# Batch 0 of an attention kernel: side blocks in pairs, one panel per output, the z and v of batch 1 fetched later, weights fetched in runs

## The chip, the core and the metric

The kernel runs on one core of a Trainium2 chip. The metric is the device time of one execution in microseconds (us). Before the change it was 1002.39 us, the median of three runs (1002.05 to 1003.09).

## The reference, cut to what matters

There are 8 batches of 3136 rows. The attention stage, which the change touches, is:

```python
scores = scale * np.matmul(z, z.transpose(0, 2, 1))   # z: 8 x 3136 x 64, scale = 1/3136
attn = np.maximum(scores, 0.0) ** 2
x = u * np.matmul(attn, v)                            # u, v: 8 x 3136 x 256
# after it, per batch: a rank-32 mixing over the rows, then relu(x @ w1) @ w2 over the channels
```

## The kernel before

The 3136 rows are 24 blocks of 128 and a tail of 64: 25 "outputs", made in the order 12 to 24, then 0 to 11. The matrix of squared scores is symmetric, so that only half of each row of blocks is computed (a "panel", thirteen blocks wide). The other half comes from panels of earlier outputs, transposed by the DMA engines into a "strip". All strips go through one queue (the sync queue), and so does the transposed copy of z for the next batch. In the trace it issues them one after another (a strip from 36.25 to 38.47 us, the two parts of z from 38.59 to 41.92, the next strip at 42.02): this is what "in-order queue" means in the prediction.

A panel part is scored on TensorE in PSUM (the memory of its results), taken out ("evicted") with a relu by ScalarE and squared by VectorE:

```python
def score(b, parts):
    ps = pair_psum()
    for k, (j, c, n, _) in enumerate(parts):
        mm(out=ps[:, k, :n], lhsT=zT[halves[k], j, :], rhs=zT_flat[halves[k], c : c + n], ...)
    # ... one or two evictions ...
    for dst, src in todo:
        nc.scalar.activation(out=dst, in_=src, func=AF.Relu, scale=sc)
    for dst, _ in todo:
        nc.vector.tensor_tensor(out=dst, in0=dst, in1=dst, op=ALU.mult)

def turn(b, o):                         # the strip of output o; five buffers
    strip = strip_pool.tile([P, HALF, P], BF16, name="strip")
    transpose(out=strip, in_=A[o][:, P:])
    strips[b, o] = strip
```

There is one array A of panels for all batches. A score of batch 1 therefore overwrites a panel of batch 0, and may do so only when everything that reads the old panel has read it, the DMA transposes among them.

Batch 0 has a start of its own, in which outputs 12 to 19 are begun before all of z is there. Its last part looks like this; the two calls in the middle are z of batch 1:

```python
rest = []
for j in reversed(range(FIRST - NG, LEAD)):                 # FIRST = 12, LEAD = 16, NG = 4
    rest += score_steps(0, j, LEAD + NG - j, NB)            # the side blocks, panel by panel
for i, pair in enumerate(pairs):
    # ...
    use_stored(pair, outs)
    if B > 1 and i in (1, 2):
        part = ((0, FIRST), (FIRST, NF))[i - 1]
        double_z(1, (part,))                                # copies on VectorE
        turn_z(1, (part,))                                  # DMA transpose on the sync queue
```

After it, tables say which panel is scored beside which output (index i is output (12 + i) mod 25, `next_at` is for the batch after), and where the loads of v of the next batch go:

```python
first_at = {8: [(NT - 2, 0, NB), (0, 0, NB)], 9: [(NT - 1, 0, NB)], 10: [(1, 0, NB)]}
first_at.update({11: [(2, 0, NB)], 12: []})
for j, i in zip(range(3, FIRST), (10, 11, 11, 12, 12, 12, 12, 12, 12)):
    first_at[i].append((j, 0, FIRST - j))
# ...
v_at = dict(zip((9, 11, 13, 15, 18, 21), V_PARTS[3:]))
```

## Time and profile before

| | before |
|---|---|
| time, median of 3 runs | 1002.39 us |
| the profiled run | 1000.08 us, span 998.3 us |
| granted TensorE clock | 1.00 |
| TensorE busy | 983.4 us, 99 % |
| idle time of TensorE | 14.9 us |

The columns are: the stretch, its length, then busy time with count of PE (TensorE), PEld (its weight loads), DVE (VectorE), ACT (ScalarE) and POOL (GpSimd), the granted TensorE clock as a share of full speed, the share of the DMA engines (the time of all packets over that of 16 engines; packets overlap, so that it can pass 1), and GB/s.

### The profile page before, as it was taken

The page shows a single profiled execution, that of the slowest core. Times are in us where ns is not written, and L with a number is a line of the kernel's source. Part 1 is how long each engine was busy: PE and PEld are TensorE (multiplying, and loading weights), DVE is VectorE, ACT ScalarE, POOL GpSimd, SP SyncE. Part 2 cuts the span into 40 slices and gives each one's busy share as a digit, 9 for nine tenths or more (in the row PEclk, how much of TensorE's full clock was granted, in tenths as well). Part 3 has the DMA queues.
Part 4 walks back from the last instruction along what each step waited for, and adds up shares of the span by engine and source line. Part 5 has one row for each costly group of instructions (what it writes and reads, how often), then busy time and mean ns, then how long its engine had stood idle before and what let it go on. Part 6 is the DMA issues. An engine that isn't in the chain of part 4 may idle for free.

```text
span 998.3 us, 31020 instructions
## 1 busy us (share of the span) xinstructions
PE 983.4 (99%) x13688; PEld 776.5 (78%) x13688; DVE 551.1 (55%) x1003; ACT 612.2 (61%) x835; POOL 171.7 (17%) x317
## 2 busy tenths in 40 slices
PE   8899999999999999999999999999999999999998
PEld 6678777787778877788787887878877788787866
DVE  6878754467444665456644566445664457542352
ACT  8877764667645776466754667556674666643154
POOL 5111112111121211221112211112111120011000
PEclk9999999999999999999999999999999999999999
DMA  9999989899798999999999997989979998678533
GB/s 195 185 195 204 174 156 186 185 176 173 153 198 171 169 157 186 179 178 169 160 180 176 181 168 149 188 174 177 175 151 194 166 188 159 120 150 161 129 95 101
DMA packets 414790, 167.94 MB, mean 168 GB/s; under 512 B 389488, under 2 KB 399408, under 8 KB 414656
## 3 DMA queue, kind: packets, MB, share of 16 engines
q1 hardware_dynamic: 385424, 99.68, 62.3%
q0 software_dynamic: 29232, 66.28, 28.3%
q8 instruction: 107, 1.75, 0.7%
q14 instruction: 27, 0.22, 0.1%
HBM read 61.88 MB, written 25.69 MB: 88 GB/s over the span
## 4 chain that ended last, share of the span: by engine, by line
PE 91%; DVE 4%; ACT 3%; DMA 1%; issue 1%; POOL 0%; DVEq 0%; POOLq 0%
PE ps L371 47%; PE ps L563 17%; PE ps L610 17%; PE ps L298 6%; ACT A L311 2%; DVE A L313 2%; PE ps L405 1%; PE ps L531 1%; DVE x_bf L545 1%; DMA out_dram<-o_sb 1%; DMA strip<-A 1%; DVE both L386 1%; PE ps L479 1%; DVE x_bf L395 1%; PE ps L207 0%
## 5 line engine op out<-in xcount | busy, mean ns | idle before, releaser
L311 ACT ACTIVATE A<-ps 128x832 bf16<-128x832 f32 (+9 forms) x477 | 358.9, 769 | 155.4 <-PE ps L298 148.1
L371 PE MATMUL ps<-v,A 64*128 64x256 bf16 x4988 | 341.6, 269 | 1.8 <-DVE A L313 1.1
L313 DVE TENSOR_TENSOR A<-A 128x832 bf16<-128x832 bf16 (+9 forms) x477 | 244.7, 527 | 133.1 <-ACT A L311 130.0
L371 PE MATMUL ps<-v,strip 64*128 64x256 bf16 x4420 | 307.3, 269 | 3.4 <-DMA strip<-A 2.5
L371 PEld LDWEIGHTS <-A 64*128 64x128 bf16 x4988 | 246.3, 94 | 45.4 <-issue 10.0
L581 ACT ACTIVATE relu_bf<-ps 128x1024 bf16<-128x1024 f32 (+2 forms) x206 | 186.2, 911 | 140.0 <-PE ps L563 139.8
L371 PEld LDWEIGHTS <-strip 64*128 64x128 bf16 x4420 | 222.6, 94 | 37.2 <-DMA strip<-A 3.9
L624 DVE TENSOR_TENSOR o_sb<-ps,x_bf 128x512 f32<-128x512 f32 (+2 forms) x105 | 69.9, 665 | 243.7 <-PE ps L610 221.7
L610 PE MATMUL ps<-w_bf,relu_bf 128*128 128x256 bf16 (+1 forms) x1600 | 201.2, 273 | 0.0
L563 PE MATMUL ps<-ut,w_bf 128*128 128x512 bf16 (+2 forms) x896 | 198.6, 353 | 0.0
L610 PEld LDWEIGHTS <-relu_bf 128*128 128x128 bf16 (+1 forms) x1600 | 153.0, 98 | 45.6 <-issue 3.6
L563 PEld LDWEIGHTS <-w_bf 128*128 128x128 bf16 x896 | 84.9, 98 | 62.0 <-issue 6.9
L355 POOL DMA_DIRECT2D u_sb<-in_u_dram x96 | 53.7, 559 | 456.1 <-DVE x_bf L395 441.9
L298 PE MATMUL ps<-zT 64*128 64x416 bf16 (+8 forms) x812 | 131.6, 312 | 0.0
L385 ACT COPY both<-ps 128x512 f32<-128x512 f32 (+1 forms) x104 | 58.9, 566 | 72.9 <-PE ps L371 66.6
L637 POOL DMA_DIRECT2D out_dram<-o_sb x84 | 46.0, 548 | 276.2 <-DVE o_sb L624 272.9
L386 DVE TENSOR_TENSOR both<-ps,both 128x512 f32<-128x512 f32 (+1 forms) x104 | 69.3, 667 | 28.2 <-ACT both L385 27.5
L395 DVE TENSOR_TENSOR x_bf<-both,u_sb 128x512 bf16<-128x512 f32 (+1 forms) x104 | 69.8, 672 | 3.7
L545 DVE TENSOR_TENSOR x_bf<-ps,x_bf 128x512 bf16<-128x512 f32 (+1 forms) x112 | 65.5, 626 | 7.2 <-PE ps L531 7.1
L298 PEld LDWEIGHTS <-zT 64*128 64x128 bf16 x812 | 43.1, 94 | 4.0
L244 POOL DMA_DIRECT2D v<-in_v_dram x61 | 34.1, 561 | 0.8 <-DMA w_bf<-in_moe_w_ch_dram 0.7
L298 PE MATMUL ps<-relu_bf 64*128 64x416 bf16 (+9 forms) x121 | 22.2, 333 | 3.9 <-ACT A L311 3.3
(54 smaller groups left out, 208.0 us busy)
## 6 DMA issues: line engine op xcount, KB each, us to landing
u_sb<-in_u_dram POOLq DMA_DIRECT2D x96, 256.0 KB, 4.1
out_dram<-o_sb POOLq DMA_DIRECT2D x84, 256.0 KB, 3.3
v<-in_v_dram POOLq DMA_DIRECT2D x57, 192.0 KB, 4.8
strip<-A SPq DMA_TRANSPOSE x196, 5.5
out_dram<-o_sb SPq DMA_DIRECT2D x11, 256.0 KB, 2.0
z_c<-in_z_dram POOLq DMA_DIRECT2D x7, 384.0 KB, 5.9
u_sb<-in_u_dram POOLq DMA_DIRECT2D x16, 64.0 KB, 2.5
ut<-x_bf SPq DMA_TRANSPOSE x56, 3.7
```

Of the source, the lines that this page charges most:

```text
L298: mm(out=ps[:, k, :n], lhsT=zT[halves[k], j, :], rhs=zT_flat[halves[k], c : c + n], start=True, stop=True,)
L311: nc.scalar.activation(out=dst, in_=src, func=AF.Relu, scale=sc)
L313: nc.vector.tensor_tensor(out=dst, in0=dst, in1=dst, op=ALU.mult)
L371: mm(out=acc[t0][h][:, (o - t0) * D : (o - t0 + 1) * D], lhsT=w[halves[h]], rhs=v_both[b % 2][halves[h], j, :], start=start, stop=stop, **kw,)
L385: nc.scalar.copy(out=both[:, :w], in_=banks[1][:, :w])
L386: nc.vector.tensor_tensor(out=both[:, :w], in0=banks[0][:, :w], in1=both[:, :w], op=ALU.add)
L395: nc.vector.tensor_tensor(out=x_at(b, t0, n), in0=split(both[:, :w]), in1=u_sb[:, :n, :].rearrange("p t (a c) -> p t a c", c=P), op=ALU.mult,)
L545: nc.vector.tensor_tensor(out=q, in0=split(ps[h][:, : len(ks) * D]), in1=q, op=ALU.add)
L563: mm(out=ps[i][:, :w] if apart else ps[:, i, :w], lhsT=w1_bf[:, db, (hp + i) * P : (hp + i + 1) * P], rhs=uT[c][:, db, len(chunks[c]) * P ...
L581: nc.scalar.activation(out=relus[c][:, hp : hp + 2, :w], in_=ps[:, :, :w], func=AF.Relu)
L610: mm(out=ps[r, k * D : (k + 1) * D], lhsT=relus[c][:, ht, q : q + (TAIL if two else P)], rhs=w2_bf[:, ht, :], start=(ht < 1 + two), stop=( ...
L624: nc.vector.tensor_tensor(out=o_sb[:p].rearrange("p t (a c) -> p t a c", c=P), in0=split(ps[:p, k0 * D : (k + 1) * D]), in1=x_at(b, t, nk) ...
```

## The change

The intent is to free the sync queue in batch 0's start, so that the strip of output 20 no longer waits behind z of batch 1, and to spread batch 0's remaining scores evenly, one panel per output. z of batch 1 is turned beside outputs 0 and 1 (i = 13 and 14), its scores start at output 3 (i = 16) and its v is loaded later. The weights w2 come in longer runs. The core of the diff (the weights' part is cut to its idea):

```diff
-        fetches = [ ... wide(w1_bf, ...), narrow, fetch, two halves of w2 ... ]
+        fetches = [first_w, narrow, fetch, second_w]     # w2 in one DMA; w1 reordered by two VectorE copies
...
-        rest = []
-        for j in reversed(range(FIRST - NG, LEAD)):
-            rest += score_steps(0, j, LEAD + NG - j, NB)
+        rest = [
+            lambda pair=pair: make_stored(pair, LEAD + NG)
+            for pair in zip(range(LEAD - 1, FIRST - NG, -2), range(LEAD - 2, FIRST - NG - 1, -2))
+        ]
...
-            if B > 1 and i in (1, 2):
-                part = ((0, FIRST), (FIRST, NF))[i - 1]
-                double_z(1, (part,))
-                turn_z(1, (part,))
...
-    first_at = {8: [(NT - 2, 0, NB), (0, 0, NB)], 9: [(NT - 1, 0, NB)], 10: [(1, 0, NB)]}
-    first_at.update({11: [(2, 0, NB)], 12: []})
-    for j, i in zip(range(3, FIRST), (10, 11, 11, 12, 12, 12, 12, 12, 12)):
+    first_at = {8 + n: [(t, 0, NB)] for n, t in enumerate((23, 24, 0, 1, 2))}
+    first_at.update({13: [], 14: []})
+    for j, i in zip(range(3, FIRST), (10, 11, 12, 13, 13, 13, 14, 14, 14)):
...
+    first_more = {8: (LEAD - 1, LEAD - 2), 9: (LEAD - 3, LEAD - 4)}
+    first_turns = {8: (23,), 9: (24,), 10: (0,), 11: (1,), 12: (2,), 13: (3, 4)}
...
+    for j, i in enumerate((16, 16, 16, 17, 17, 18, 19, 19, 20, 21, 22, 23)):
+        after_first[i].append((j, FIRST - j, NB))
...
-        v_at = dict(zip((9, 11, 13, 15, 18, 21), V_PARTS[3:]))
+        v_at = dict(zip((15, 16, 18, 19, 21, 22), V_PARTS[3:]))
...
+                if b == 0 and i == 12:
+                    double_z(b + 1, ((FIRST, NF), (0, FIRST)))
-                if b and i == 7:
+                if i == (7 if b else 13):
                     turn_z(b + 1, ((FIRST, NF),))
-                if b and i == 10:
+                if i == (10 if b else 14):
                     turn_z(b + 1, ((0, FIRST),))
-                if i == 11:
+                if i == (11 if b else 15):
                     extend_z(b + 1)
```

More of the change, by code (lines that the diff above doesn't have):

```diff
@@ L252, in weight_steps, with first_w, second_w, order_w @@
     def weight_steps():
-        def wide(w_bf, w):
-            pool_dma(out=w_bf, in_=w.rearrange("(t p) d -> p t d", p=P))
+        w1_tmp = x_bf[:, NC - 1 :, :].rearrange("p a h -> p (a h)")
+        w1_tmp = w1_tmp[:, : ND * H].rearrange("p (a h) -> p a h", a=ND)
+        def first_w():
+            pool_dma(out=w1_tmp, in_=moe_w_ch1.rearrange("(t p) d -> p t d", p=P))
+        def second_w():
+            pool_dma(out=w2_bf, in_=moe_w_ch2.rearrange("(p t) d -> p t d", t=NH))
+        def order_w(a):
+            nc.vector.tensor_copy(
+                out=w1_bf[:, a, :].rearrange("p (t q) -> p t q", q=P),
+                in_=w1_tmp[:, a, :].rearrange("p (q t) -> p t q", t=NH),
+            )
         def narrow():
@@ L276, in copies @@
                 nc.vector.tensor_copy(out=V_bf[n : 2 * n, :], in_=V_bf[:n, :])
-        fetches = [
-            lambda: wide(w1_bf, moe_w_ch1),
-            narrow,
-            fetch,
-            lambda: wide(w2_bf[:, NH // 2 :, :], moe_w_ch2[H // 2 :, :]),
-            lambda: wide(w2_bf[:, : NH // 2, :], moe_w_ch2[: H // 2, :]),
-        ]
+        fetches = [first_w, narrow, fetch, second_w]
         third = FIRST // 2
         puts = [lambda t=t: put(t, t + third) for t in range(0, NF, third)]
-        return fetches, puts + [put_tail, copies]
+        orders = [lambda a=a: order_w(a) for a in range(ND)]
+        return fetches, puts + [put_tail, copies] + orders
     strips = {}
@@ L663, in beside, with make_stored @@
             begun.add((t0, h))
+    def make_stored(pair, first, n=NG):
+        todo = []
+        for j in pair:
+            k0, k1 = first - j, min(NB, first + n - j)
+            todo.append((j, first * P, (k1 - k0) * P, A[j][:, k0 * P : k1 * P]))
+        score(0, todo)
     def start_up():
@@ L758, in use_stored @@
                         beside(o, j, block(0, o, j))
-        def make_stored(pair):
-            todo = []
-            for j in pair:
-                k0, k1 = LEAD - j, min(NB, LEAD + NG - j)
-                todo.append((j, LEAD * P, (k1 - k0) * P, A[j][:, k0 * P : k1 * P]))
-            score(0, todo)
-        nxt += [lambda pair=pair: make_stored(pair) for pair in pairs[:2]]
+        nxt += [lambda pair=pair: make_stored(pair, LEAD) for pair in pairs[:2]]
         run(nxt[:2])
@@ L781, in start_up @@
             if i + 2 < len(pairs):
-                make_stored(pairs[i + 2])
+                make_stored(pairs[i + 2], LEAD)
             else:
@@ L818 @@
         own_at[i].append((j, 0, FIRST - j))
-    first_at = {8: [(NT - 2, 0, NB), (0, 0, NB)], 9: [(NT - 1, 0, NB)], 10: [(1, 0, NB)]}
-    first_at.update({11: [(2, 0, NB)], 12: []})
-    for j, i in zip(range(3, FIRST), (10, 11, 11, 12, 12, 12, 12, 12, 12)):
+    first_at = {8 + n: [(t, 0, NB)] for n, t in enumerate((23, 24, 0, 1, 2))}
+    first_at.update({13: [], 14: []})
+    for j, i in zip(range(3, FIRST), (10, 11, 12, 13, 13, 13, 14, 14, 14)):
         first_at[i].append((j, 0, FIRST - j))
-    first_turns = {8: (NT - 2,), 9: (NT - 1, 0)}
+    first_more = {8: (LEAD - 1, LEAD - 2), 9: (LEAD - 3, LEAD - 4)}
+    first_turns = {8: (23,), 9: (24,), 10: (0,), 11: (1,), 12: (2,), 13: (3, 4)}
     next_at = {i: [] for i in range(NT)}
@@ L830 @@
         next_at[i].append((FIRST + j, 0, NB))
+    after_first = {i: [] for i in range(NT)}
+    for j, i in enumerate((16, 16, 16, 17, 17, 18, 19, 19, 20, 21, 22, 23)):
+        after_first[i].append((j, FIRST - j, NB))
+    for j, i in enumerate((16, 17, 18, 20, 21, 22, 24)):
+        after_first[i].append((FIRST + j, 0, NB))
     def run(steps):
@@ L837 @@
     start_up()
-    puts = dict(zip((13, 14, 15, 16, 17, 18), puts))
+    puts = dict(zip((13, 14, 15, 16, 17, 18, 19, 20), puts))
     late = []
@@ L850 @@
             fill = [s for key in own.get(i, ()) for s in score_steps(b, *key)]
+            if b == 0 and i in first_more:
+                fill.append(lambda pair=first_more[i]: make_stored(pair, LEAD + 2 * NG))
             if more:
-                fill += [s for key in next_at[i] for s in score_steps(b + 1, *key)]
+                coming = next_at if b else after_first
+                fill += [s for key in coming[i] for s in score_steps(b + 1, *key)]
                 if b and i == 1:
                     load_z(b + 1, WHOLE)
-                if b and i == 7:
+                if b == 0 and i == 12:
+                    double_z(b + 1, ((FIRST, NF), (0, FIRST)))
+                if i == (7 if b else 13):
                     turn_z(b + 1, ((FIRST, NF),))
-                if b and i == 10:
+                if i == (10 if b else 14):
                     turn_z(b + 1, ((0, FIRST),))
```

## The prediction

> **What bounds the kernel now.** I read the page's busy shares first, then the busy time in 6 us stretches of batch 0, then the waits of the weight loads, and last the timelines of the sync queue, ScalarE and the weight loads.
>
> ```profile
> PE 983.4 (99%) x13688; PEld 776.5 (78%) x13688; DVE 551.1 (55%) x1003; ACT 612.2 (61%) x835; POOL 171.7 (17%) x317
> ```
>
> TensorE is busy 99% of the span of 998.3 us: 14.9 us idle in all. Whatever the change does can come only out of idle or slowed time of TensorE. The stretches (columns: PE, PEld, DVE, ACT, POOL busy with counts, clock, DMA share, GB/s) show that it all lies early:
>
> ```profile
> 30.00:36.00 6.00, 6.00 (x104) 5.13 (x106) 5.54 (x16) 5.40 (x11) 0.00 (x0) 1.00 1.02 164
> 36.00:42.00 6.00, 5.74 (x77) 3.99 (x74) 4.45 (x8) 5.84 (x9) 0.00 (x0) 1.00 1.13 210
> 42.00:48.00 6.00, 3.62 (x63) 3.24 (x62) 5.32 (x12) 4.62 (x9) 1.61 (x3) 1.00 1.29 194
> 48.00:54.00 6.00, 5.48 (x96) 4.55 (x97) 2.06 (x4) 3.73 (x5) 0.00 (x0) 1.00 1.11 186
> 54.00:60.00 6.00, 5.09 (x89) 4.22 (x85) 4.50 (x9) 4.41 (x7) 1.62 (x3) 1.00 1.22 184
> 60.00:66.00 6.00, 5.45 (x93) 3.18 (x90) 5.20 (x12) 5.66 (x11) 1.09 (x2) 1.00 1.22 205
> 66.00:72.00 6.00, 6.00 (x114) 5.25 (x112) 3.19 (x8) 3.69 (x8) 1.58 (x2) 1.00 1.23 249
> ```
>
> From 66 us on TensorE is never idle in batch 0; between 36 and 66 us it idles 4.6 us, and in 36:42 it is "busy" 5.74 us with only 77 matmuls while ScalarE is busy 5.84 of 6: there it is slowed by the scores' eviction. What the idle time waits for stands in the weight loads, which wait on behalf of their matmuls:
>
> ```profile
> PEld L371 <- DMA strip<-A: 3.9, 2, 2.8
> ...
> 48.52 0.22 PEld L371 LDWEIGHTS <-strip 64*128 64x128 bf16 x6 [2.76 <-DMA strip<-A]
> ...
> 57.55 0.09 PEld L371 LDWEIGHTS <-strip 64*128 64x128 bf16 x1 [1.19 <-DMA strip<-A]
> ```
>
> Both waits are for transposed strips of A (outputs 20 and 23). The sync queue shows why they are late:
>
> ```profile
> 29.84 8.63 SPq L333 DMA_TRANSPOSE strip<-A  x4
> 38.59 3.33 SPq L195 DMA_TRANSPOSE zT<-z_bf  x2
> 42.02 34.23 SPq L333 DMA_TRANSPOSE strip<-A  x12
> ```
>
> ```profile
> 42.02 6.45 DMA strip<-A
> ```
>
> The second fence is from the chain of waits: the strip of output 20 is issued at 42.02 and lands at 48.47, and TensorE goes on at 48.52. Ahead of it in the same in-order queue stand the two transposes of batch 1's z.
>
> [...] the issue at 42.02 is over at 45.06 and the data is there at 48.47. [...] the DMA share is 1.0 to 1.3 throughout. [...] the strided copies of V, 768 wide, take 0.82 us each here (0.94 elements per ns)[...].
>
> **The change, part by part.**
>
> (a) *z's two transposes leave the queue ahead of strip 20.* Strip 20 then takes the place of the first of them: issued at 38.59, landing when that one landed, near 42.8 (issue plus its 4.25). All strips behind it move up some 5 to 6 us. Both strip waits, 2.76 and 1.19 us, should go.
>
> (b) *Side blocks in pairs.* Before, the side blocks of eight panels were done whole around 39 to 44 us: 1024, 896, 768 ... 128 columns, 4608 in all. After, only the part for outputs 20 to 23 is done there, two panels in one PSUM pair (3328 columns), and 1280 columns follow beside outputs 20 and 21. One eviction of 832 columns starts 0.76 us after the last, one of 512 costs about 0.5. ScalarE loses about 1.1 us there and gains it back where it has room. TensorE's work from strip 16's first block (35.49 us) to strip 20's is 8.3 us before (halves at 24 in 1.31 us, a pair of 416 columns 0.18 us) and took 10.55 us to 46.04, so 2.2 us were lost to eviction. After it is 8.0 us. ScalarE's new work there sums to about 7.1 us from 36.31, so it hardly binds: I take 1 us of loss. Strip 20's first block comes at about 44.5 instead of 48.52: 4 us gained.
>
> (c) *Panels one per output, batch 1's scores later.* From output 20 to the first score of batch 1, TensorE has 22.3 us of work by the order of the built program; 2% of small losses (the rate of 66 to 97 us before) and the 64-row output make it 23.1. It would reach that score at 67.6. The kernel before has done the same amount of work at about 73.8. If nothing new waits, the change is worth 6 us. Total matmul work is equal (4 matmuls fewer); by about 97 us both have done the same.
>
> (d) *The new wait.* In the changed order the sync queue holds: strip 2, z part, strip 3, strip 4, z part, with no other wait of weight ahead of the z parts than strip 2's. Strip 2 needs panel 2's squares, now made beside output 24. Output 24 starts at about 55.8; the second half of the panel is scored halfway through, evicted by 58.4; VectorE meanwhile has the sums of outputs 22 and 23 (0.68 + 0.69) and four copies of z (0.62 + 1.07 = 1.69 us, a duration of before) in front of the squares, which end at about 60.7. So the second z part is the fifth of a burst of five from 60.7. The only such burst in the trace starts at 29.84 and its fifth (the first z part) lands at 42.84, 13 us later; with no load beside it. Taking 12 to 13 us, it lands at 72.7 to 73.7, while TensorE wants it at 67.6 for the first score beside output 3: a new wait of 5.1 to 6.1 us. That leaves 73.2 against 73.8, or 0.6 us gained.
>
> (e) *v of batch 1 later, w2 in runs, w1 reordered.* The v loads move from outputs 21 to 8 to outputs 2 to 9: six in eight outputs, each 0.97 us of the DMA engines (as they land one after another at 27 to 29 us). With a strip at about 2.2 us and u, that is near 3.3 us per output of 3.1 us: the strips lose perhaps 2 us of the 4 to 5 us that they have in hand. Nothing on the path. w2's bytes are the same; its two halves took 1.3 us each, the rate of v's long runs, so nothing there. w1's two strided copies take about 1024/0.94 = 1.1 us each on a VectorE that is half idle: nothing.
>
> Sum: -6.2 (a to c) +5.5 (d) = about -0.7 us, and I allow for a hidden part of d: 1002.4 - 1.4 = 1001.0.
>
> **Rivals.**
> 1. *The z parts arrive in time.* For it: z transposes of later batches take 4.2 us to land, and if the squares of panel 2 or the burst are 3 us quicker each, the wait is gone. Against: even four issues ahead of it at their shortest, 1.44 us, and 4.2 us to land make 60.7 + 5.8 + 4.2 = 70.7, still 3 us late. It would gain all 6 us: 996.
> 2. *The DMA engines bind.* The later v loads meet the z burst; u and v loads beside transposes stretched strips to 8 to 9.8 us to landing at 69 to 92 us before. For it: VectorE's copy that extends z stands in its in-order stream and holds up the sums too. Against: while TensorE waits for z, the strips get ahead. It would make 1003 to 1005.
> 3. *ScalarE binds at outputs 4 to 9*, where batch 1's scores are pressed together: output 9 has 3072 columns, about 3.1 us with its copies against 3.3 us on TensorE. It costs 0 to 1 us.
>
> **Range and chances.** Centre 1001.0 us; 996.5 (no z wait) to 1005.0 (z wait with DMA crowding). 2% is 20 us, more than all idle time of TensorE, and no part of the change adds work: faster 0.01, within 2% 0.98, slower 0.01.
>
> **What would show it.** Right: no wait for strips at outputs 20 and 23, strip 20's first block at 44 to 45.5 us; one new wait of 3 to 7 us on TensorE near 68 us for the transposed z (its weight load), with five transposes in a row on the sync queue; nothing after 75 us. Wrong: strip waits still there at 44 to 58 us (a fails); no z wait (d fails, about 996); idle TensorE at 75 to 100 us with strips landing late (e fails, up to 1005).

The sum came to -6.2 + 5.5 = -0.7 us, and with the allowance for a hidden part of (d) to 1001.0 us.

## More of the kernel before

The prediction shows the lines on which it rests. Two more are needed to compare with later. They are the busy time in two stretches of the kernel before.

```profile
72.00:78.00 6.00, 6.00 (x110) 5.08 (x106) 5.72 (x10) 4.84 (x7) 0.58 (x1) 1.00 1.36 191
78.00:84.00 6.00, 6.00 (x110) 5.12 (x106) 4.53 (x9) 3.88 (x6) 1.11 (x2) 1.00 1.11 173
```

TensorE is busy all the time here, at full clock, with 110 matmuls in 6 us. That is the normal pace.

## The result, and the profile after

| | before | changed |
|---|---|---|
| median of 4 runs | 1002.74 us | 1007.89 us |
| range | 1002.05 to 1004.11 | 1006.99 to 1009.36 |
| the profiled run | 1000.08 us, span 998.3 | 1009.36 us, span 1007.7 |
| mean granted clock | 1.00 | 0.995 |

The ratio is 1.0050, with a 95 % interval of 1.0035 to 1.0066. A ratio here is the mean time of one kernel's fast runs over that of the other's of the same rounds, so it is not quite the ratio of the medians. The changed kernel is half a per cent slower. It is within 2 %, as predicted, but outside the predicted range (996.5 to 1005.0), and on the other side of the kernel before.

**Where the time went.** The matmul records can be added up to an amount of work done. One unit here is 2400 columns of a full 128-row, 128-column matmul, and a matmul that uses half of the array counts for half (in the traces 24 of these of 256 columns take 1.31 us, 0.055 us each, and 20 full ones of 512 columns 4.37 us, 0.22 us each). The times at which the two profiled runs have done the same work are:

| units of matmul work | before, us | changed, us | changed minus before |
|---|---|---|---|
| 20 | 30.81 | 31.11 | +0.30 |
| 45 | 64.05 | 58.34 | -5.71 |
| 50 | 69.87 | 66.22 | -3.65 |
| 55 | 74.98 | 81.25 | +6.27 |
| 60 | 80.00 | 87.07 | +7.07 |
| 100 | 121.47 | 128.50 | +7.03 |

The changed kernel gains 6 us up to unit 45, loses 12.8 us between units 45 and 60, and nothing more up to unit 100. (The two profiled runs end 9.4 us apart and the medians 5.2 us. From unit 100 to unit 250 the two traces stay 7.0 us apart; the other 2.3 us come, net, in single steps after that, in stages that the change does not touch and with the clock at 1.00 in both. I have no explanation for them.)

Page of the changed kernel, busy time of the engines:

```profile
PE 983.5 (98%) x13684; PEld 782.7 (78%) x13684; DVE 553.4 (55%) x1009; ACT 612.3 (61%) x839; POOL 170.1 (17%) x316
```

TensorE's busy time is the same to 0.1 us, while the span is 9.4 us longer: in sum, the loss is idle time. The stretches, columns as above:

```profile
42.00:48.00 6.00, 6.00 (x105) 5.42 (x103) 5.29 (x15) 5.61 (x11) 1.08 (x2) 1.00 1.16 192
...
60.00:66.00 6.00, 3.61 (x68) 3.27 (x66) 5.05 (x12) 3.19 (x6) 1.08 (x2) 1.00 0.81 168
66.00:72.00 6.00, 4.36 (x84) 4.08 (x77) 2.94 (x7) 1.25 (x3) 1.10 (x2) 1.00 1.09 144
72.00:78.00 6.00, 0.00 (x0) 0.00 (x0) 0.00 (x0) 0.00 (x0) 0.00 (x0) 0.54 1.21 204
78.00:84.00 6.00, 5.01 (x60) 3.83 (x62) 2.22 (x6) 2.19 (x5) 0.00 (x0) 0.61 1.27 200
84.00:90.00 6.00, 6.00 (x108) 5.46 (x106) 5.65 (x13) 5.42 (x9) 1.65 (x3) 1.00 0.74 146
```

The hole of 42 to 48 us (3.62 us busy before) is filled. In its place is a stretch, 72 to 78 us, in which no compute engine does anything while the DMA engines are full (1.21). The granted clock then falls to 0.54 and 0.61, so that 5.01 us of "busy" TensorE hold only 60 matmuls. The waits between 30 and 110 us (what waits, for whom, us in total, times, longest) name the cause:

```profile
PE ps L307 <- DMA zT<-z_bf: 8.6, 1, 8.6
...
ACT both L400 <- DVE both L395: 2.4, 1, 2.4
PE ps L307 <- ACT A L320: 2.4, 1, 2.4
```

The timeline of TensorE shows both waits, and what the lower clock does:

```profile
63.80 0.28 PE L307 MATMUL ps<-relu_bf 64*128 64x256 bf16 x2 [2.39 <-ACT A L320]
...
69.75 0.62 PE L380 MATMUL ps<-v,A 64*128 64x256 bf16 x8
78.99 0.24 PE L307 MATMUL ps<-zT 64*128 64x64 bf16 x2 [8.62 <-DMA zT<-z_bf]
79.03 1.26 PE L380 MATMUL ps<-v,A 64*128 64x256 bf16 x10
...
82.75 0.71 PE L380 MATMUL ps<-v,strip 64*128 64x256 bf16 x10
```

TensorE runs dry at about 70.4 and goes on at 78.99, when the second part of z of batch 1 has been transposed. The ten matmuls at 79.03 take 1.26 us, those at 82.75 take 0.71: it works at about half speed for some 3.7 us after the wait. The granted clock was 0.50 from 72.4 to 82.7 us (0.54 and 0.61 in the two stretches): it fell 2.0 us after TensorE had run dry. v_mix_again below compares two waits, of which only one was followed by half clock.

The sync queue (start, time in issue, form and count):

```profile
62.63 1.97 SPq L195 DMA_TRANSPOSE zT<-z_bf  x1
64.69 7.64 SPq L342 DMA_TRANSPOSE strip<-A  x2
72.37 2.15 SPq L195 DMA_TRANSPOSE zT<-z_bf  x1
```

It is the burst of five that the prediction named: the strip of output 2 issued at 61.25, a z part, two strips, the other z part. It starts at 61.25 and its last data is there at 78.94, 17.7 us later. GpSimd's loads of u and v of 64.13, 64.66, 69.67 and 70.23 land beside it.

The earlier wait, 2.39 us at 61 to 64, comes from VectorE. First VectorE, then ScalarE:

```profile
58.58 1.61 DVE L188 COPY z_bf<-z_c 128x832 bf16<-128x832 bf16 x4
60.10 1.62 DVE L322 TENSOR_TENSOR A<-A 128x832 bf16<-128x832 bf16 x3
61.64 0.42 DVE L395 TENSOR_TENSOR both<-ps,both 128x256 f32<-128x256 f32 x1
```

```profile
62.09 0.82 ACT L400 COPY both<-both 64x256 f32<-64x256 f32 x2 [2.41 <-DVE both L395]
```

The sum of the tail output (L395) stands behind the four copies of z and three squares in VectorE's stream. ScalarE waits 2.41 us for it, with the next eviction of scores behind it in its own stream, and TensorE waits for that eviction.

### The profile page after: what moved, and what is told of

It is laid out like the page before. It is cut to its first block, busy times and chain, and to the rows that moved or that the text cites. A ratio compares the mean times of both kernels' runs of the same rounds, so it can differ in the third digit from the quotient of the medians.

```text
span 1007.7 us, 31023 instructions
## 1 busy us (share of the span) xinstructions
PE 983.5 (98%) x13684; PEld 782.7 (78%) x13684; DVE 553.4 (55%) x1009; ACT 612.3 (61%) x839; POOL 170.1 (17%) x316
## 3 DMA queue, kind: packets, MB, share of 16 engines
q1 hardware_dynamic: 385424, 99.68, 61.2%
q0 software_dynamic: 28320, 66.28, 28.0%
## 4 chain that ended last, share of the span: by engine, by line
PE 87%; DVE 4%; DMA 3%; issue 2%; ACT 2%; POOL 1%; SPq 0%; DVEq 0%; POOLq 0%; ACTq 0%
PE ps L380 46%; PE ps L619 16%; PE ps L572 16%; PE ps L307 7%; DVE A L322 2%; DMA out_dram<-o_sb 2%; ACT A L320 1%; DMA zT<-z_bf 1%; PE ps L414 1%; PE ps L540 1%; DVE x_bf L554 1%; DVE both L395 1%; DMA z_c<-in_z_dram 1%; DVE x_bf L404 1%; PE ps L488 1%
## 5 line engine op out<-in xcount | busy, mean ns | idle before, releaser
L380 PEld LDWEIGHTS <-A 64*128 64x128 bf16 x4988 | 249.8, 94 | 43.4 <-issue 10.4
L380 PEld LDWEIGHTS <-strip 64*128 64x128 bf16 x4420 | 226.0, 94 | 30.9
L395 DVE TENSOR_TENSOR both<-ps,both 128x512 f32<-128x512 f32 (+1 forms) x104 | 69.4, 667 | 28.7 <-ACT both L394 28.0
```

What stands on the lines that cost most here:

```text
L380: mm(out=acc[t0][h][:, (o - t0) * D : (o - t0 + 1) * D], lhsT=w[halves[h]], rhs=v_both[b % 2][halves[h], j, :], start=start, stop=stop, **kw,)
L395: nc.vector.tensor_tensor(out=both[:, :w], in0=banks[0][:, :w], in1=both[:, :w], op=ALU.add)
```

## The experiments

There were sixteen runs of fifteen kernels, in four groups of four, each group on one chip with its own runs of the kernel before, five rounds each. "At 45, 60, 100" is the time in us at which the profiled run had done so many units of work. Some traces lack 40 matmul records, all of a later stage (the channel product) and all but one of them after unit 100, so these early times are complete but for 0.2 us at unit 100. Times at unit 20 vary by about 1 us between executions (30.78 to 31.74, and 32.85 for v_old, whose clock was at half from 8.8 to 12.2 us), so that differences under 1 us mean nothing here.

| kernel | median us (range) | ratio to before, 95 % interval | at 45 | at 60 | at 100 |
|---|---|---|---|---|---|
| before | 1002.27, 1001.54, 1002.26, 1002.64 in the four groups | 1 | 64.05 | 80.00 | 121.47 |
| changed | 1007.89 (1006.99 to 1009.36) | 1.0050, 1.0035 to 1.0066 | 58.34 | 87.07 | 128.50 |
| z_early | 1007.01 (1004.76 to 1019.32) | 1.0067, 1.0027 to 1.0106 | 64.27 | 80.89 | 124.60 |
| z_spread | 1003.26 (1001.01 to 1003.79) | 1.0004, 0.9990 to 1.0018 | 59.71 | 77.75 | 123.53 |
| v_old | 1007.99 (1006.00 to 1009.96) | 1.0053, 1.0039 to 1.0068 | 61.71 | 87.66 | 129.31 |
| warm | 1008.21 (1005.94 to 1016.28) | 1.0068, 1.0039 to 1.0097 | 59.22 | see text | see text |
| spread_v | 1006.03 (1001.28 to 1014.21) | 1.0046, 1.0010 to 1.0081 | 61.09 | 80.52 | 122.88 |
| before_z | 1002.08 (1000.75 to 1009.03) | 1.0010, 0.9980 to 1.0041 | 61.21 | 83.62 | 125.08 |
| dbl_early | 1007.28 (1004.53 to 1008.28) | 1.0048, 1.0027 to 1.0070 | 59.61 | 84.39 | 125.82 |
| w_old | 1009.45 (1007.85 to 1014.09) | 1.0082, 1.0056 to 1.0109 | 59.39 | 87.19 | 128.62 |
| after_no_v | 1005.90 (1002.65 to 1011.29) | 1.0019, 0.9965 to 1.0074 | 58.77 | 83.29 | 124.94 |
| spread_no_v | 998.51 (996.70 to 1001.37) | 0.9946, 0.9899 to 0.9992 | 58.82 | 76.90 | 118.55 |
| later_a | 1002.26 (997.59 to 1013.33) | 0.9980, 0.9923 to 1.0037 | 59.85 | 77.72 | 122.82 |
| v_mix | 1000.03 (998.70 to 1002.07) | 0.9959, 0.9914 to 1.0005 | 60.01 | 81.34 | 122.98 |
| v_mix_again | 1001.02 (999.85 to 1003.47) | 0.9987, 0.9965 to 1.0010 | 59.65 | 80.33 | 121.97 |
| v_mix2 | 1003.49 (1001.66 to 1009.50) | 1.0028, 0.9997 to 1.0059 | 59.01 | 81.85 | 123.50 |
| mix2_later | 1003.80 (997.31 to 1006.80) | 1.0007, 0.9977 to 1.0038 | 59.02 | 81.50 | 123.15 |
| pairs_only | 1006.23 (1001.47 to 1015.27) | 1.0042, 1.0002 to 1.0083 | 67.32 | 83.94 | 125.81 |

**Theory after the result:** the 12.8 us are lost to the late second part of z, in three terms: the transfer itself (8.6), the half clock after it (1.3 to 2.1) and VectorE held up by z's copies (2.4). The transfer is so late because loads of u and v lie beside the burst. **Rivals:** the scores of batch 1, pressed together, cost the time by themselves; the weights' new order does; the transposes are slow by themselves, whatever lies beside them.

### First group: z back, z sooner, v back, and the clock

**z_early** puts z's copies and transposes of batch 1 back into the start-up stage, and keeps the rest of the change.

```diff
+            if B > 1 and i in (1, 2):
+                part = ((0, FIRST), (FIRST, NF))[i - 1]
+                double_z(1, (part,))
+                turn_z(1, (part,))
...
-                if b == 0 and i == 12:   # and turn_z at 13 and 14
+                                         # taken out
```

> The changed kernel with the two z copies and z transposes of batch 1 put back where the kernel before has them, ahead of strip 20; pairs, panels, later scores, later v and w2 stay. If the place of the z transposes is the cause of the loss (my theory): no wait for z, TensorE's clock 1.00 throughout, the old wait for strip 20 near 44 to 48 us is back (3 to 4 us), time 1000 to 1002.5, that is 5 to 8 us below the changed kernel. If the later v loads or the later, denser scores are the cause (rivals): the loss stays, 1006 or more.

It took 1007.01 us: a miss. The trace lost what the change had gained before unit 45 (64.27), as it must, and had no wait for z. But the clock did not stay at 1.00: the wait for strip 20, 2.98 us that ended at 48.65, was followed by 3.4 us of half clock.

```profile
48.00:54.00 6.00, 5.26 (x61) 3.81 (x63) 0.82 (x3) 1.84 (x3) 0.00 (x0) 0.72 1.10 236
```

And a wait came that the kernel before does not have. Waits between 70 and 102 us:

```profile
ACT A L320 <- DMA strip<-A: 2.8, 1, 2.8
PE ps L307 <- ACT A L320: 1.9, 1, 1.9
```

ScalarE waits to put a score of batch 1 into panel 8, because the transposed strip of batch 0 that still reads panel 8 is late. Two loads of v stand beside it. In the kernel before, strip 8 landed at 85.69 us and the score that overwrites its panel came at 87.66, 2 us after it.

**z_spread** keeps the change, but copies z at output 21 (i = 9) and turns it beside outputs 22 and 23 (i = 10 and 11), each part between two strips.

```diff
-                if b == 0 and i == 12:
+                if b == 0 and i == 9:
                     double_z(b + 1, ((FIRST, NF), (0, FIRST)))
-                if i == (7 if b else 13):
+                if i == (7 if b else 10):
-                if i == (10 if b else 14):
+                if i == (10 if b else 11):
```

> The changed kernel with z doubled beside output 21 and its two transposes put singly between strips 24 and 0 and between strips 0 and 1, where the sync queue is idle half of the time. Theory: neither the old strip wait nor the z wait nor the half clock, strip 20's first block at 44.6 us as in the changed kernel, time 995.5 to 997.5. Rival (v loads or dense scores cost): 1001 or more, with idle TensorE after 70 us.

The wait for z went away, the clock stayed at 1.00, and it is 0.5 % faster than the changed kernel: the late z is the cause of the loss (the wait, the half clock after it and most of the wait for VectorE, 0.86 us instead of 2.39, are removed together). But the time, 1003.26 us, is the rival's: it did not keep the 4 us that it had gained. At unit 60 it was 2.3 us ahead of the kernel before, at unit 100 2.1 us behind. ScalarE, then TensorE:

```profile
87.93 2.78 ACT L320 ACTIVATE A<-ps 128x576 bf16<-128x576 f32 x4 [3.46 <-DMA strip<-A]
...
92.50 6.22 ACT L320 ACTIVATE A<-ps 128x640 bf16<-128x640 f32 x8 [1.31 <-DMA strip<-A]
```

```profile
88.63 0.35 PE L307 MATMUL ps<-zT 64*128 64x416 bf16 x2 [2.57 <-ACT A L320]
...
93.26 0.35 PE L307 MATMUL ps<-zT 64*128 64x416 bf16 x2 [1.21 <-ACT A L320]
```

It is the wait of z_early again, larger. The strips issued at 78.75 and 82.06 needed 9.1 and 10.4 us to land, against the 5.4 us median of all strips in the changed kernel, with v loads at 78.07, 78.60 and 84.59 beside them. The changed kernel has no such wait; as I read it, its strips catch up while TensorE waits for z.

**v_old** keeps the late z and puts the v loads back where the kernel before has them.

```diff
-        v_at = dict(zip((15, 16, 18, 19, 21, 22), V_PARTS[3:]))
+        v_at = dict(zip((9, 11, 13, 15, 18, 21), V_PARTS[3:]))
```

> The changed kernel with the v loads of batch 1 back at outputs 21, 23, 0, 2, 5 and 8; z stays late. Theory (five transposes in one burst, which the loads only stretch): the second z part still lands late, at 73 to 76 us instead of 78.9, the z wait shrinks from 8.6 to 3 to 6 us, time 1002 to 1005. Rival (the v loads are the cause): the z wait is gone or under 1.5 us, time below 999.

It took 1007.99 us, a miss: the wait for z fell from 8.6 to 4.5 us, but TensorE also waited 1.4 us for a strip, and the clock dipped twice (0.72 in 66 to 72 us and in 78 to 84). Its profiled run was already 1.7 us later than that of the changed kernel at unit 20, after the half clock in its start-up; from unit 20 to unit 100 it took 96.5 us, against 97.4.

**warm** puts 38 unread matmuls of 512 columns in front of the first score of batch 1, to keep TensorE busy while it waits.

```diff
+    def warm():
+        ps = pair_psum()
+        for _ in range(38):
+            rhs = v_both[0][:, :2, :].rearrange("p t d -> p (t d)")
+            mm(out=ps[:, 0, :], lhsT=eye, rhs=rhs, start=True, stop=True)
...
+            if b == 0 and i == 16:
+                fill[0] = lambda s=fill[0]: (warm(), s())
```

> The changed kernel with 38 matmuls of 512 columns that nobody reads, put right ahead of the first score of batch 1, so that TensorE works through about 8.1 us of the z wait. The result stays right. Theory: the z part lands as late as before, but the clock stays at 1.00 after it, where it was 0.54 to 0.61 from 72 to 84 us; 1.5 to 2.2 us are saved, time 1005.5 to 1006.5. If the low clock costs nothing beyond the wait: same as the changed kernel, 1007.5 to 1008.5.

```profile
72.00:78.00 6.00, 6.00 (x29) 2.74 (x28) 0.00 (x0) 0.00 (x0) 0.00 (x0) 1.00 1.24 251
78.00:84.00 6.00, 6.00 (x92) 4.41 (x91) 3.44 (x8) 3.48 (x7) 0.00 (x0) 1.00 1.21 191
```

The clock stayed at 1.00, and 78 to 84 us held 92 matmuls instead of 60. The second z part was there at 78.45 us, so that the added matmuls, which held TensorE until 79.48, cost 1.0 us themselves. From there to unit 100, with their 8.1 units taken off, it took 48.2 us, and the changed kernel 49.5 us from its first score of batch 1 on: 1.3 us for the clock. Two other readings give more. The changed kernel worked at half clock from 78.99 to 82.67 us, which loses half of 3.7 us, 1.8 us; and it loses 9.92 + 0.80 = 10.7 us between units 50 and 60 with a wait of 8.6, which leaves 2.1 us. The timed runs do not show it (1008.21 us), so the size is from one trace of each only.

### Second group: the parts alone

**spread_v** is z_spread with v's loads back at their old places.

```diff
-        v_at = dict(zip((15, 16, 18, 19, 21, 22), V_PARTS[3:]))
+        v_at = dict(zip((9, 11, 13, 15, 18, 21), V_PARTS[3:]))
```

> The changed kernel with three things moved: z of batch 1 copied at output 21 instead of 24, its two transposes beside outputs 22 and 23 (between strips 24, 0 and 1) instead of 0 and 1, and the loads of v of batch 1 back to where the kernel before has them (outputs 21, 23, 0, 2, 5, 8). Theory (two costs, each from its own move: the late z, and the late dense v loads that delay the strips which batch 1's scores wait to overwrite): no z wait at 68 to 80, clock 1.00 there, no ScalarE wait for strips at 84 to 100, and 996 to 998.5 us against 1002.3. Rival (TensorE's order of work is simply too tight for the DMA engines whichever load is moved): a wait for strips or for z turns up elsewhere before 80 us and the time stays at 1001 to 1004.

1006.03 us, the rival. The profiled run was good (1001.28 us), but TensorE waited four times for strips between 36 and 73 us, 4.4 us in all, now that v loads stood beside the z transposes. Three of the six runs were longer (1006.95 to 1014.21 us), with a clock of 0.994 to 0.997.

**before_z** is the kernel before with z alone moved: copies at output 20, transposes beside outputs 21 and 22.

```diff
-            if B > 1 and i in (1, 2):  # z of batch 1 in the start-up
...
+                if b == 0 and i == 8:
+                    double_z(b + 1, ((FIRST, NF), (0, FIRST)))
-                if b and i == 7:
+                if i == (7 if b else 9):
-                if b and i == 10:
+                if i == 10:
-                if i == 11:
+                if i == (11 if b else 12):
```

> The kernel before with one part of the change alone: the copies of z of batch 1 and its transposes taken out of the start-up stage (copies beside output 20, transposes beside outputs 21 and 22, that is behind strips 23 and 24). Theory (part a of the prediction: the two strip waits of 2.8 and 1.2 us before outputs 20 and 23 are worth what they last): strip waits gone, 998 to 1000 us. Rival (the gain is given back in the same stage to the eviction of the side blocks, or later to z): 1001 to 1003, with the time at equal matmul work ahead at 50 us and not at 80.

1002.08 us, no difference from the kernel before (1001.54). The two strip waits were gone and the trace was 2.8 us ahead at unit 45. Then (waits between 30 and 110 us):

```profile
ACT both L391 <- DVE both L386: 6.7, 1, 6.7
DVE zT L238 <- DMA zT<-z_bf: 6.0, 1, 6.0
...
PE ps L298 <- DMA zT<-z_bf: 3.5, 1, 3.5
```

VectorE's copy that extends z (it repeats the first twelve blocks behind the last) waited 6.0 us for the transfer, with the sums of the tail output behind it, and TensorE waited 3.5 us; the clock was 0.50 from 66 to 72 us. Part (a) of the prediction is worth its strip waits only where z does not come late for it.

**dbl_early** is the changed kernel with z's copies at output 21 instead of 24, the transposes unmoved.

```diff
-                if b == 0 and i == 12:
+                if b == 0 and i == 9:
                     double_z(b + 1, ((FIRST, NF), (0, FIRST)))
```

> The changed kernel with z's four copies moved from output 24 to output 21, the transposes where the change has them. Theory (of the z wait, some 2.4 us come from VectorE, where the copies stand ahead of panel 2's squares and the sum that the tail output waits for): the 2.4 us wait at 61 to 64 is gone, the strip of output 2 goes out about 1.5 us earlier, but the z part is still behind a burst and TensorE still waits for it for 5 to 8 us, because it also wants it earlier: 1004.5 to 1007. Rival (the copies set the burst): z lands before 74, wait under 4 us, 1001 to 1003.

```profile
63.54 0.29 PE L307 MATMUL ps<-relu_bf 64*128 64x256 bf16 x2 [0.86 <-ACT A L320]
76.69 0.24 PE L307 MATMUL ps<-zT 64*128 64x64 bf16 x2 [6.58 <-DMA zT<-z_bf]
```

The wait at 61 to 64 us shrank from 2.39 to 0.86 us, as expected, and it comes from the copies. The z wait shrank to 6.58 us, but not as I had thought: the burst began only 0.25 us sooner (61.00 instead of 61.25) and was shorter, 15.6 us instead of 17.7, with the same loads beside it. At unit 60 it was 2.7 us better than the changed kernel. The time, 1007.28 us, is inside what was expected but does not differ from the changed kernel's.

**w_old** is the changed kernel with the weights loaded as before.

```diff
-        fetches = [first_w, narrow, fetch, second_w]
+        fetches = [ ... wide(w1_bf, ...), narrow, fetch, two halves of w2 ... ]
-        return fetches, puts + [put_tail, copies] + orders
+        return fetches, puts + [put_tail, copies]
```

> The changed kernel with w1 and w2 loaded and placed as in the kernel before (w2 in two halves, w1 straight to its place, no reordering copies on VectorE). Theory (the weights are not on the path): no difference from the changed kernel, 1006 to 1009. Rival (w2's runs or w1's copies move VectorE and the DMA engines at 60 to 100 us and cost the later strips): 1003 to 1005.

1009.45 us, not faster than the changed kernel, and its trace is at 87.19 at unit 60 and 128.62 at unit 100, like it, though by another way: the wait for VectorE was followed by half clock from 66.2 to 69.6 us, and the z wait was 5.65 us, with a burst of 16.4 us. Nothing shows the weights on the path. (The profiled run ends 4.7 us later than that of the changed kernel. It is level with it up to unit 210 and loses the time after that, in stages that the change does not touch.)

### Third group: the loads beside the burst

**after_no_v** is the changed kernel without the six late loads of v of batch 1. That part of v is zero instead, so the result is wrong.

```diff
+            for t in range(9, NT):
+                nc.gpsimd.memset(v_both[1][:, t, :], 0.0)      # in the start-up
...
-                if b == 0 and i in v_at:
-                    load_v(b + 1, v_at[i])
```

> The changed kernel without the six late loads of v of batch 1 (that part of v is set to zero early, on GpSimd; wrong result on purpose). It shows what these loads do to the burst of five transposes and to the strips. Theory (the burst takes 17.7 us instead of the 12 to 13 expected because u and v loads share the DMA engines with it): the second part of z lands 12 to 14 us after the burst begins, TensorE's wait for z shrinks from 8.6 to 3 to 5 us, no ScalarE wait for strips later; 1001 to 1004 us. Rival (the sync queue's transposes are slow by themselves, or wait for other things): the burst still takes 16 us or more, the wait stays at 7 to 9 us, 1006 to 1008.

```profile
64.22 0.28 PE L307 MATMUL ps<-relu_bf 64*128 64x256 bf16 x2 [2.38 <-ACT A L320]
75.35 0.20 PE L307 MATMUL ps<-zT 64*128 64x64 bf16 x2 [4.56 <-DMA zT<-z_bf]
```

The burst began at 61.68 and ended at 75.33 with VectorE's and TensorE's going on: 13.7 us, where it had been 17.7. The wait fell from 8.62 to 4.56 us. But the burst is not always as long with the loads: the four traces that have them at the change's places show 17.7 (changed), 16.4 (w_old), 16.3 (warm) and 15.6 us (dbl_early). So two v loads (192 KB each) beside the burst cost 2 to 4 us, measured against a single trace without them, and the rest is the length of the burst with two loads of u still beside it, which the prediction had at 12 to 13 us. At unit 60 it is 3.8 us better than the changed kernel. The timed gain is 2 us by the medians, 1005.90 (outside the 1001 to 1004 expected) against 1007.89, in different groups and with wide ranges. (The page of the changed kernel puts the packets of both queues down to the same 16 engines: 61.2 % of their time for q1, the sync queue's, and 28.0 % for q0, whose 66.28 MB are GpSimd's loads and stores.)

**spread_no_v** is z_spread without these loads, wrong in the same way.

```diff
 # z_spread, and as in after_no_v:
-                if b == 0 and i in v_at:
-                    load_v(b + 1, v_at[i])
```

> The kernel with z copied at output 21 and turned beside outputs 22 and 23, without the six late loads of v of batch 1 (zeros instead, wrong result on purpose). Theory (the DMA engines are what bounds 48 to 95 us, and the lead of 4 us is lost to v loads wherever they stand): no waits of TensorE or ScalarE for strips from 48 to 100 us, time at 100 units of matmul work 4 us or more ahead of the kernel before, 995 to 998.5 us. Rival (TensorE's lead is lost to something else, such as VectorE's squares or the evictions): at 100 units of work under 2 us ahead, 1000 us or more.

998.51 us, in the expected range of time and 0.54 % faster than the kernel before by the ratio (0.4 % by the medians: the kernel before had runs of 1012.21 and 1015.14 us in this group, which lower every ratio of it). No ScalarE wait for strips was left, and TensorE's waits for strips from 30 to 110 us were 1.7 us. It reached unit 100 2.9 us ahead of the kernel before, less than the 4 us that I had asked for: between units 50 and 75 it lost 1.6 us, 1.3 of it in one wait for a strip.

**later_a** is z_spread with the scores that overwrite panels 8 to 11 one output later.

```diff
-    for j, i in enumerate((16, 16, 16, 17, 17, 18, 19, 19, 20, 21, 22, 23)):
+    for j, i in enumerate((16, 16, 16, 17, 17, 18, 19, 19, 21, 22, 23, 24)):
```

> The kernel with z copied at output 21 and turned beside 22 and 23, and the scores of batch 1 that overwrite panels 8 to 11 put one output later each (everything else the same, v loads late). Theory (the 3.8 us of waits at 84 to 95 are ScalarE waiting to overwrite panels 8 and 9 that late strips still have to read): ScalarE's wait for strips under 1 us, TensorE's wait for ScalarE gone; 999 to 1001.5. Rival (strips late for TensorE too): waits of TensorE for strips take their place, 1002 to 1004.

1002.26 us. TensorE's wait for ScalarE fell from 4.6 to 1.3 us, but its waits for strips rose from 1.6 to 4.2 us, 2.3 us of it at 90 to 102 us: the rival. ScalarE's own wait for strips, expected under 1 us, was 4.9 us, as in z_spread (4.8). The strips themselves are late, and the overwritten panels are only the first to feel it.

**v_mix** is z_spread with the v loads spread over outputs 21, 24, 2, 4, 7 and 9.

```diff
-        v_at = dict(zip((15, 16, 18, 19, 21, 22), V_PARTS[3:]))
+        v_at = dict(zip((9, 12, 15, 17, 20, 22), V_PARTS[3:]))
```

> The same kernel with z spread, and the v loads of batch 1 at outputs 21, 24, 2, 4, 7 and 9, so that none lies beside the z transposes and only three lie between 60 and 85 us. Theory (where the v loads stand decides which strips are late): waits under 2 us in all from 48 to 100 us, 998 to 1001. Rival (the DMA engines are full all along and any place costs the same): 1002 to 1006, waits of 3 us or more.

1000.03 us in the median and all six runs between 998.70 and 1002.07, as the theory expected for the time. The theory's condition (waits under 2 us) did not hold: TensorE still waited 4.0 us for strips.

### Fourth group: what was still open

**v_mix2** has v at outputs 24, 2, 4, 7, 9 and 10.

```diff
+        v_at = dict(zip((12, 15, 17, 20, 22, 23), V_PARTS[3:]))
```

> z copied at output 21 and turned beside 22 and 23; v loads of batch 1 at outputs 24, 2, 4, 7, 9 and 10 (the kernel v_mix had one at 21 instead of the one at 10). Theory (each transfer moved into a stretch with room removes its own wait): the strip wait of 1.3 us near 54 us, which came with the load at output 21, is gone; 998 to 1000 us. Rival (the wait moves on): waits for strips near 85 to 95 us instead, 1000 to 1002.

1003.49 us, a miss. The strip wait at 54 us was gone, but one of 3.7 us came at 72 us, with the clock at 0.72 after it.

**mix2_later** is v_mix2 with the later scores of later_a.

```diff
+        v_at = dict(zip((12, 15, 17, 20, 22, 23), V_PARTS[3:]))
+    for j, i in enumerate((16, 16, 16, 17, 17, 18, 19, 19, 21, 22, 23, 24)):
```

> The same as v_mix2, with the scores of batch 1 that overwrite panels 8 to 11 one output later each. Theory (overwriting waits still cost something at 80 to 95 us): 1 us or less faster than v_mix2, 997 to 999.5. Rival (no wait left there, or later scores crowd batch 1's first outputs): the same or up to 2 us slower than v_mix2.

1003.80 us against 1003.49: no difference, the rival. The runs from 997.31 to 1006.80 do not allow more.

**pairs_only** is the changed kernel with both z and v at the places of the kernel before: z_early and v_old in one.

```diff
 # z_early, and:
+        v_at = dict(zip((9, 11, 13, 15, 18, 21), V_PARTS[3:]))
```

> The changed kernel with z and v of batch 1 both where the kernel before has them: pairs, one panel per output, and batch 1's scores from output 3 on are what is left of the change. Theory (z and v's places cause the loss, the rest costs nothing): strip waits of 3 to 4 us at outputs 20 and 23 as before, no ScalarE wait for strips at 84 to 95; 1001 to 1003.5, like the kernel before. Rival (batch 1's scores pressed into outputs 3 to 11 cost by themselves): ScalarE's wait to overwrite panels still 2 us or more at 84 to 95, 1004 to 1007.

1006.23 us: the time is the rival's, the trace is the theory's with a cost that I had not counted. ScalarE did not wait for strips at all from 84 to 95 us, and from unit 60 to unit 100 the kernel lost 0.4 us to the kernel before. So the pressed scores of batch 1 cost nothing by themselves. The loss came earlier:

```profile
49.00 1.05 PE L380 MATMUL ps<-v,strip 64*128 64x256 bf16 x16 [2.89 <-DMA strip<-A]
...
53.30 0.39 PE L380 MATMUL ps<-v,strip 64*128 64x256 bf16 x1 [2.10 <-DMA strip<-A]
53.30 1.45 PE L380 MATMUL ps<-v,A 64*128 64x256 bf16 x10
```

The strip waits of the kernel before are back, a little longer, and here the clock fell to 0.67 and 0.76 between 48 and 60 us, where it was 1.00 before. With pairs, TensorE does its work sooner, and then waits for the same transfers.

**v_mix_again** repeats v_mix on another chip.

```diff
 # v_mix, unchanged
```

> The kernel v_mix once more on this chip. Theory (its gain is real): 998.5 to 1001, ratio 0.996 to 0.999 with an interval below 1. Rival (disturbed runs of the kernel before made it): ratio 0.999 or more.

1001.02 us against 1002.64; the ratio is 0.9987, but the interval reaches 1.0010. So v_mix is 0.6 to 0.9 % faster than the changed kernel by the ratios to before, and at best 0.1 to 0.4 % faster than the kernel before (0.2 % by the medians of both groups), with both intervals reaching past 1: better than the change, and not shown to be better than what was there. The two traces of v_mix differ in one thing. First the one, then the other:

```profile
71.72:75.13 3.41, 1.31 (x24) 1.12 (x26) 0.52 (x2) 0.67 (x2) 0.00 (x0) 1.00 1.28 182
75.13:78.54 3.41, 3.41 (x34) 2.27 (x32) 2.17 (x4) 2.56 (x4) 0.00 (x0) 0.50 1.12 115
```

```profile
63.25:66.66 3.41, 2.11 (x36) 1.83 (x35) 2.79 (x6) 1.85 (x4) 1.08 (x2) 1.00 1.29 99
66.66:70.08 3.42, 2.19 (x44) 1.97 (x46) 0.52 (x2) 1.24 (x3) 0.00 (x0) 1.00 1.16 237
70.08:73.49 3.41, 1.91 (x38) 1.47 (x34) 3.33 (x5) 0.01 (x1) 1.10 (x2) 1.00 1.29 179
```

Both have a wait of 2.2 us for a strip, from 71.6 to 73.8 us in the first and from 65.7 to 67.9 us in the second (which has another of 1.5 us behind it). In the first trace half clock followed (0.50 from 75.13 to 78.54 us), in the second the clock stayed at 1.00. The length of the wait does not tell the two apart. Nor does it elsewhere: the waits of 2.48 us for strip 20 in the kernel before and of 2.39 us for VectorE in the changed kernel were followed by full clock (1.00 in 48 to 54 and in 66 to 72 us), and the wait for VectorE in w_old, 2.4 us too, by half clock (0.72 in 66 to 72 us). What differs between the two traces of v_mix is how the wait lies in the stretches shown. They are 3.41 us long, as long as the half clock of the first trace, and in that trace one of them ends where the clock fell. Nearly the whole wait lies in that one, which leaves TensorE busy for 1.31 us of it; in the second trace the wait is split over two, with 2.11 and 2.19 us busy, and the third has 1.91. In the changed kernel TensorE was busy for 1.34 us of the 3.41 us before the clock fell (69.02 to 72.43 us). That the place of a wait decides, and not its length alone, is my reading of these few stretches; how long TensorE has to idle for half clock to follow is not shown. (The ends of matmuls are modelled in the traces, so that the busy times are rough.)

## Why the prediction was wrong, by its own steps

- **(a) z out of the way of strip 20: right.** Strip 20's first block came at 44.59 us, predicted 44 to 45.5; the waits at outputs 20 and 23 are gone.
- **(b), (c) pairs and panels, 6 us ahead: right up to unit 45** (5.7 to 6.0 us ahead). Then the first wait for VectorE, 2.39 us, took part of it back. TensorE wanted the first score of batch 1 at 70.4 us instead of 67.6. The prediction had counted z's four copies as a delay of the squares, and had not asked who else stands behind them: the sum of the tail output. dbl_early showed it.
- **(d) the new wait: the mechanism was right, its size is the step that failed.** "Taking 12 to 13 us, it lands at 72.7 to 73.7" was taken from a burst "with no load beside it" (but for one of u that landed 1.5 us into it). With the loads of u and v beside it the burst took 17.7 us and the part landed at 78.94 (15.6 to 16.4 us in three other traces with the same loads); without those of v it took 13.7 us (after_no_v). So the term was 8.6 us instead of 5.1 to 6.1, although TensorE came to it 2.8 us later than predicted; the part landed 5 to 6 us late.
- **What a wait costs beyond its length was missing.** The sum had no term for the clock. It was 1.3 (by warm) to 2.1 us (by the table of work done).
- **(e) v later, "nothing on the path": wrong.** The loads made the burst 2 to 4 us longer. "Nothing after 75 us" did hold in the changed kernel for units 60 to 100, but that was luck, as far as the traces tell: z_spread, without the wait, lost 4.3 us between units 60 and 100. That w2 and w1 cost nothing was right as far as w_old shows.
- **The sum:** -6.2 + 5.5 was predicted; measured from unit 20 on, -6.0 + 2.1 (VectorE) + 9.9 and 0.8 (the wait, the clock) = +6.8 us in the trace.
- **Rival 2** (the v loads meet the z burst, 1003 to 1005) named the right cause, including VectorE's extending copy that waits for the transfer, and I gave it too little weight and too small a size. I had set "strips get ahead while TensorE waits" against it, which fits the traces and is not the point.

What stays open: the timed differences and the traces at unit 100 agree only to 2 to 4 us. At unit 100 the traces of dbl_early and warm are 2.7 and 0.8 us better than that of the changed kernel and their times are not. Each kernel but v_mix has a single trace, and of v_mix's two traces only one has half clock after its wait of 2.2 us.

## What to carry to other kernels

A transfer that is moved off one path has to be placed on another: before moving it, list every load that will be issued beside it, and take the duration of a burst only from a burst with the same neighbours. Making TensorE faster in one stage may only move its wait to where the transfers are late, as in pairs_only (waits of 2.89 and 2.10 us for strips, with a DMA share of 1.19 in 48 to 54 us). Count a wait of TensorE with the half-clock time that may follow it (here 3.41 us after a wait of 2.2 us in v_mix and 10.24 us with the wait of 8.6 us in the changed kernel, but none after 2.48 us in the kernel before), and look in each engine's stream for who stands behind an instruction that is moved or waits.
